# Starting three gate and value products of block 1 on three of its four tiles, and loading q and k of the next tiles ahead of the output weights

## The chip, the cores and the metric

The kernel runs on one core of a Trainium2 chip. The metric is the device time of one execution in microseconds (us): the median of three runs. A lower time is better. The core has a matrix engine (PE, with its weight loads shown apart as PEld), a vector engine (DVE), an activation engine (ACT), GpSimd (POOL), whose queue issues most of the loads here, and SyncE (SP), which issues stores and transposing transfers.

## The reference

An attention with a sliding window and a linear bias over the distance feeds a gated feed-forward block. The output of the attention, for 8 sequences of 576 tokens with 8 heads of 64, becomes a matrix x of 4608 tokens by 512.

```python
window = 128
scale = 1.0 / np.sqrt(D)
scores = scale * np.matmul(q, k.transpose(0, 1, 3, 2))
bias = slopes[:, None, None] * (-np.abs(rel))[None, :, :]
mask = (rel >= 0) & (rel < window)
scores = np.where(mask, scores + bias[None], -1e9)
attn = softmax(scores)                      # written out in the reference
x = np.matmul(attn, v)                      # then 4608 x 512
g = x @ w_gate                              # 512 x 1536
silu = g * (1.0 / (1.0 + np.exp(-g)))
out = (silu * (x @ w_val)) @ w_out          # 1536 x 512
```

## The kernel before

The tokens are cut into tiles of 128 (`unit` i, tile i), and four tiles make a block of 512 tokens, nine blocks in all. Attention works tile by tile, and the feed-forward part works block by block, some steps behind it. The two are written as generators that are advanced in turn, so that instructions of both alternate on each engine.

A tile of k or q is loaded by the POOL queue, turned on PE through the identity (`pt`, line 214) and copied out of PSUM by ACT (k) or DVE (q). Scores (`ps`, `psc`) take the turned k and q, ACT takes their exponential, DVE multiplies by the mask, and PE weighs v with it (`av`, line 350). DVE divides by the sum into `x`, PE turns `x` (`px`, line 376), and ACT copies it into `xT[n]`, the input of block n.

The gate and value products of a block are made by `wide`. Each has four matmuls over the 512 rows of the input, on up to 512 tokens of the block. A product can be done in two goes: first on the columns of the tiles that are there, and later on the rest, in the same PSUM buffer. The kernel before uses that for block 0 alone. The PSUM pool `ps_f` has three buffers under the tag `gv`.

```python
def wide(n, m, which, c1=512):                       # line 394
    w, ms = wg_sb if which == "g" else wv_sb, slice(m * P, (m + 1) * P)
    ps, c0 = early.pop((n, m, which), (None, 0))
    if ps is None:
        pool, tag = (ps_a, "a") if (n, m, which) in OTHER else (ps_f, "gv")
        ps = pool.tile([P, 512], FP32, name="p" + which, tag=tag)
    for kb in range(NKB):                            # 4
        nc.tensor.matmul(ps[:, c0:c1], w[:, kb, ms], xT[n][:, kb, c0:c1], ...)   # line 402
    if c1 < 512:
        early[(n, m, which)] = (ps, c1)
    return ps

def gate(n, m, pg, ...):                             # frees the gate's buffer
    nc.scalar.activation(tt, pg, AF.Tanh, scale=0.5)                   # line 420, ACT
    nc.vector.scalar_tensor_tensor(out=uu, in0=tt, ..., in1=pg, ...)   # line 421, DVE

def val(n, m, pv, ...):                              # frees the value's buffer
    nc.vector.tensor_mul(hT[n][:, m, ...], uu, pv)                     # line 432, DVE

def project(n, j, pool, tag, bufs):                  # output product of block 0, tile j
    po = pool.tile([P, DM], FP32, name="po", tag=tag, bufs=bufs)
    for m0 in range(0, NMB, 4):
        for i in range(m0, m0 + 4):
            m = NMB - 1 - i if n == 0 else i
            nc.tensor.matmul(po, hT[n][:, m, ...], wo_sb[:, m, :], ...)   # line 456
        ...
```

`project` for block 0 reads the second half of the output weights `wo_sb` first (m from 11 down). Its first tile has 12 matmuls, of which the first six use `wo_sb[:, 6:12]` and the others `wo_sb[:, 0:6]`. It follows the last product of block 0 in the program, while tiles 7 and 8 of the attention are under way. The feed-forward generator and the order of loads, cut:

```python
def ffn():
    for n in range(NBLK):
        ...
        if n == 1:
            for j in range(PRE):                     # PRE = 0
                ...
        for m in range(NMB):                         # 12
            for half, _ in enumerate(gate_val(n, m)):
                ...
            if n == 1:
                if m in (4, 6, 8, 10):
                    for _ in project(0, m // 2 - 2, ps_f, "po", 1):
                        yield 1.0
# ... cut ...
def begin(n, tiles):
    for m, which in ((0, "g"), (0, "v"), (1, "g"), (1, "v"), (2, "g"), (2, "v"))[:n]:
        if early.get((0, m, which), (None, 0))[1] < tiles * P:
            wide(0, m, which, tiles * P)
# ... cut: the loads, in the order of the POOL queue ...
load_w(1280, 1536)
load_v(7)
load(8)
nc.gpsimd.dma_start(wo_sb[:, 6:12, :], wo2[:, 6:12, :])
nc.gpsimd.dma_start(wo_sb[:, 0:6, :], wo2[:, 0:6, :])
load_qk(9)
load_qk(10, "q")
load_v(9)
load_qk(10, "k")
load_v(10)
```

The place of an instruction in its engine's queue is not that of the source alone: a list scheduler orders PE, DVE and ACT. The POOL queue keeps the order of the source.

Of the kernel before, what the change touches and what calls it, by code (L numbers as in the profile page):

```python
# [16 lines left out]
P = 128  # L17
# [33 lines left out]
def kernel(  # L51
# [117 lines left out]
    def source(src, rank):  # L169

        s, c = divmod(rank, 9)
        if c == 8:
            return [((64 * n, 64 * n + 64),
                     src[2 * s + n, :, 512:576, :].rearrange("h p d -> p h d")) for n in range(2)]
        b, t = 2 * s + c // 4, c % 4
        return [((0, P), src[b, :, t * P:(t + 1) * P, :].rearrange("h p d -> p h d"))]

    def load_v(rank):
        va[rank] = va_all[rank % NV]
        for (p0, p1), src in source(v, rank):  # L180
            nc.gpsimd.dma_start(va[rank][p0:p1, :, 0:D], src)  # L181

    def load_qk(rank, which="kq"):
        for name in which:
            t_ = nat.tile([P, H, D], FP16, name=name + "n", tag=name + "n")
            for (p0, p1), src in source(k if name == "k" else q, rank):
                nc.gpsimd.dma_start(t_[p0:p1], src)  # L187
            (natk if name == "k" else natq)[rank] = t_

    def load(rank):  # L190
        load_qk(rank)
        load_v(rank)
# [198 lines left out]
    early = {}  # L391
    OTHER = {(0, 0, "g"), (0, 0, "v"), (0, 1, "g"), (0, 1, "v")}

    def wide(n, m, which, c1=512):
# [6 lines that stand above are left out]
        for kb in range(NKB):  # L401
            nc.tensor.matmul(ps[:, c0:c1], w[:, kb, ms], xT[n][:, kb, c0:c1],  # L402
                             start=(kb == 0 and c0 == 0), stop=(kb == NKB - 1 and c1 == 512),
                             skip_group_check=(n == 0))
        if c1 < 512:
            early[(n, m, which)] = (ps, c1)
        return ps
# [26 lines left out]
    def gate_val(n, m):  # L434
        c0 = 384 if (n, m) in acted else 0
        gate(n, m, wide(n, m, "g"), c0)
        yield
        val(n, m, wide(n, m, "v"), c0)
        yield
# [11 lines left out]
    def project(n, j, pool, tag, bufs):  # L451
# [4 lines that stand above are left out]
                nc.tensor.matmul(po, hT[n][:, m, j * P:(j + 1) * P], wo_sb[:, m, :],  # L456
                                 start=(i == 0), stop=(i == NMB - 1))
            if m0 + 4 == NMB:
                osb = opool.tile([P, DM], FP32, name="osb", tag="osb")
                nc.scalar.mul(osb, po, 0.5)  # L460
                store(n, j, osb)
            yield
# [10 lines left out]
    def weight_sums(c):  # L473

        if c == 0:
            one_more.append(supool.tile([P, 1], FP32, name="one", tag="pin", bufs=1))
            nc.vector.memset(one_more[0], 1.0)
        k = slice(2 * c, 2 * c + 2)
        for t_, a, b in ((T1, B12, B11), (T3, B22, B12)):
            nc.vector.scalar_tensor_tensor(out=t_[:, k, :], in0=a[:, k, :], scalar=one_more[0],  # L480
                                           in1=b[:, k, :], op0=ALU.mult, op1=ALU.subtract)
        nc.vector.tensor_sub(T2[:, k, :], B22[:, k, :], T1[:, k, :])
        nc.vector.tensor_sub(T4[:, k, :], B21[:, k, :], T2[:, k, :])
# [11 lines left out]
    def at_once(fs):  # L495
        for f in fs:
            f()
# [208 lines left out]
    def ffn():  # L706

        for n in range(NBLK):
            if n > 1:
                parts = chain(strassen(n - 1, 0), strassen(n - 1, 1))  # L710
            if n == 1:
                for j in range(PRE):
                    for _ in project(0, j, ps_f, "po", 1):
                        yield 1.0
            if n == SEVEN_FROM:
                break
            due, given = 0, 0
            for m in range(NMB):
                for half, _ in enumerate(gate_val(n, m)):
                    scored[0] = False  # L720
                    yield 1.0
                    due += n > 1 and 2 * m + half in AT
                    while due and not (scored[0] and given % 7 == 1):
                        next(parts)
                        due, given = due - 1, given + 1
                        yield 0.75
                    if n > 1:
                        for _ in range(1 + (len(later) > 3)):
                            if later:
                                later.pop(0)()  # L730
# [4 lines that stand above are left out]
                    if m in (4, 6, 8):  # L735
                        weight_sums(m // 2 - 2)
                if n > 0 and m >= 9:
                    (at_once if n == 1 and m < 11 else later.extend)(sums(n, m - 9))
                if n + 1 == SEVEN_FROM:
                    if m == SILU_AT:  # L740
                        attention_ends()
                        by_silu.update((n, i) for i in range(m + 1, NMB))
                    if m in (SILU_AT + 1, SILU_AT + 2):
                        later.extend(gate_val_weight_sums(m - SILU_AT - 1))
                    if m == SILU_AT:
                        later.extend(x_sums(n + 1))
            if n > 1:
                assert next(parts, 0) == 0
        ends = [strassen(NBLK - 1, t) for t in range(2)]
        tail = ExitStack()  # L750
        for n, k, name, which in seven_steps():
            if k == 0 and n > SEVEN_FROM:
                assert next(parts, 0) == 0
                parts = chain(strassen(n - 1, 0), strassen(n - 1, 1))
            if n == SEVEN_FROM and k in (1, 3, 10, 17):
                later.extend(gate_val_weight_sums(2 + (k + 4) // 7))
            yield 0.5
            if k % 3 == 2 and k < 42:
                next(parts)
                yield 0.75  # L760
            if k == 20 and n + 1 < NBLK:
                later.extend(x_sums(n + 1))
            if k == 35:
                later.extend(sums(n, 0))
            if name == "fourth" and which is not None and which[1] > 3:
                if n + 1 < NBLK or k < 39:
                    later.extend(sums(which[0], which[1] - 3))
            for _ in range(2 if len(later) > 4 or k < 7 else 1):
                if later:
                    later.pop(0)()  # L770
            if n == NBLK - 1 and k == 38:
                at_once(later)
                later.clear()
                tail.enter_context(tc.manual_schedule(engines={ET.DVE}))
            if n == NBLK - 1 and k == 39:
                one, two = sums(n, 1), sums(n, 2)
                one[0]()
            if n == NBLK - 1 and k == 41:
                one[1]()
                next(ends[0])  # L780
                yield 0.75
            if n == NBLK - 1 and k == 42:
                two[0]()
        assert next(parts, 0) == 0 and not later
        at_once((two[1], one[2], two[2], one[3], two[3]))

        for t in (1, 0, 1, 0, 1, 0, 1, 0, 0, 1, 0, 1, 1):
            next(ends[t])
            yield 0.75
        tail.close()  # L790
# [25 lines left out]
                f()  # L816
            yield

    def begin(n, tiles):

        for m, which in ((0, "g"), (0, "v"), (1, "g"), (1, "v"), (2, "g"), (2, "v"))[:n]:
            if early.get((0, m, which), (None, 0))[1] < tiles * P:
                wide(0, m, which, tiles * P)

    def first_tiles():

# [83 lines left out]
    load_w(1280, 1536)  # L910
    load_v(7)
    load(8)
    nc.gpsimd.dma_start(wo_sb[:, 6:12, :], wo2[:, 6:12, :])
    nc.gpsimd.dma_start(wo_sb[:, 0:6, :], wo2[:, 0:6, :])
    load_qk(9)
    load_qk(10, "q")
    load_v(9)
    load_qk(10, "k")
    load_v(10)
# [94 lines left out]
```

The softmax here doesn't subtract the row's maximum and nothing guards it: scores larger than these inputs give would overflow.

## Time and profile before

| what | value |
|---|---|
| device time, median of 3 runs | 340.84 us (340.82 to 340.93) |
| span of the profiled execution | 339.4 us |
| PE busy | 328.6 us, 97% of the span |
| DVE busy | 274.7 us, 81% |
| ACT busy | 208.3 us, 61% |
| POOL busy | 109.7 us, 32% |

The page of the profile gives the busy time of each engine first, then the same in 40 slices of 8.5 us, each digit a share in tenths. The view of waits sums, for each instruction of an engine, the idle time before it by what ended it. The timeline lists instructions in order with start, duration and idle time before. A matmul's duration includes the passage through the array, which overlaps with the next matmul. So the pace of PE is read from the distance of two starts, and not from durations.

### The profile page before, as it was taken

The page shows a single profiled execution, that of the slowest core. Times are in us where ns is not written, and L with a number is a line of the kernel's source. Part 1 is how long each engine was busy: PE and PEld are TensorE (multiplying, and loading weights), DVE is VectorE, ACT ScalarE, POOL GpSimd, SP SyncE. Part 2 cuts the span into 40 slices and gives each one's busy share as a digit, 9 for nine tenths or more (in the row PEclk, how much of TensorE's full clock was granted, in tenths as well). Part 3 has the DMA queues.
Part 4 walks back from the last instruction along what each step waited for, and adds up shares of the span by engine and source line. Part 5 has one row for each costly group of instructions (what it writes and reads, how often), then busy time and mean ns, then how long its engine had stood idle before and what let it go on. Part 6 is the DMA issues. An engine that isn't in the chain of part 4 may idle for free.

```text
span 339.4 us, 7672 instructions
## 1 busy us (share of the span) xinstructions
PE 328.6 (97%) x2935; PEld 217.4 (64%) x2935; DVE 274.7 (81%) x643; ACT 208.3 (61%) x415; POOL 109.7 (32%) x136
## 2 busy tenths in 40 slices
PE   8999987999999999999999999999999999999994
PEld 4564444444455665566665655666688888888884
DVE  4668874999888779998899999999955885776683
ACT  4866774555575676666665647563467776776650
POOL 8977675377837068743008000000000000000000
PEclk9999999999999999999999999999999999999998
DMA  9999999999999999999939913021101101011014
GB/s 151 169 178 178 166 162 162 128 139 157 142 170 147 172 153 179 157 156 154 181 109 109 152 39 93 17 58 53 62 2 64 47 17 65 0 65 62 2 64 125
DMA packets 160037, 37.37 MB, mean 110 GB/s; under 512 B 147328, under 2 KB 155648, under 8 KB 160000
## 3 DMA queue, kind: packets, MB, share of 16 engines
q0 software_dynamic: 118336, 18.62, 80.3%
q1 hardware_dynamic: 40976, 17.64, 28.4%
q10 hardware_dynamic: 688, 0.62, 0.6%
q8 instruction: 23, 0.38, 0.5%
q14 instruction: 14, 0.11, 0.1%
HBM read 37.91 MB, written 9.44 MB: 139 GB/s over the span
## 4 chain that ended last, share of the span: by engine, by line
PE 79%; DMA 11%; POOL 4%; DVE 2%; ACT 2%; issue 1%; POOLq 0%
PE po L537 19%; PE pg L402 15%; PE pv L402 15%; PE gX L626 9%; DMA wv_sb<-in_moe_w_val_dram 5%; PE gY L626 5%; PE av L350 4%; DMA qn<-in_q_dram 3%; PE ps L282 3%; PE p L537 3%; DMA va<-in_v_dram 3%; PE gZ L626 2%; PE po L456 2%; POOL va L181 1%; PE px L376 1%
## 5 line engine op out<-in xcount | busy, mean ns | idle before, releaser
L402 PE MATMUL pv<-xT,wv_sb 128*128 128x512 f16 (+2 forms) x304 | 75.8, 368 | 0.3 <-DVE uu L421 0.3
L402 PE MATMUL pg<-xT,wg_sb 128*128 128x512 f16 (+2 forms) x304 | 75.1, 368 | 0.2 <-DVE xT L378 0.2
L420 ACT ACTIVATE tt<-pg 128x512 f16<-128x512 f32 x68 | 41.0, 603 | 47.2 <-PE pg L402 46.9
L288 ACT ACTIVATE ex<-ps 128x512 f16<-128x512 f32 x96 | 49.9, 606 | 7.5 <-PE ps L282 7.5
L421 DVE SCALAR_TENSOR_TENSOR uu<-tt,pg 128x512 f16<-128x512 f16 x67 | 45.6, 680 | 9.1 <-ACT tt L420 9.1
L432 DVE TENSOR_TENSOR hT<-uu,pv 128x512 f16<-128x512 f16 x68 | 46.2, 680 | 2.9 <-PE pv L402 1.3
L181 POOL DMA_DIRECT2D va<-in_v_dram x40 | 34.3, 865 | 42.3 <-PE av L350 34.6
L537 PEld LDWEIGHTS <-hT 128*128 128x128 f16 x384 | 37.2, 98 | 10.6 <-issue 0.8
L402 PEld LDWEIGHTS <-wv_sb 128*128 128x128 f16 x304 | 27.3, 98 | 24.8 <-issue 2.7
L402 PEld LDWEIGHTS <-wg_sb 128*128 128x128 f16 x304 | 27.3, 98 | 23.2 <-issue 1.9
L187 POOL DMA_DIRECT2D kn<-in_k_dram x39 | 33.3, 858 | 16.8 <-DMA qT<-qn 6.4
L187 POOL DMA_DIRECT2D qn<-in_q_dram x39 | 33.4, 865 | 12.6 <-DMA va<-in_v_dram 5.4
L537 PEld LDWEIGHTS <-S 128*128 128x128 f16 x288 | 27.4, 98 | 7.3 <-issue 1.4
L294 DVE TENSOR_TENSOR ex<-ex,m_reg 128x1024 f16<-128x1024 f16 x42 | 28.7, 685 | 2.6 <-ACT ex L288 2.5
L353 DVE TENSOR_TENSOR x<-av,rec 128x256 f16<-128x256 f32 x72 | 28.7, 419 | 0.4
L537 PE MATMUL po<-T,S 128*128 128x256 f16 x192 | 25.9, 273 | 0.3 <-ACT u2s L563 0.3
L537 PE MATMUL po<-T,hT 128*128 128x256 f16 x192 | 26.0, 272 | 0.0
L322 ACT ACTIVATE exc<-psc 128x512 f16<-128x512 f32 x40 | 21.3, 607 | 1.9 <-PE psc L318 1.9
L680 DVE TENSOR_TENSOR hT<-s,v 128x512 f16<-128x512 f16 x18 | 7.6, 424 | 17.7 <-ACT s L679 17.7
L350 PEld LDWEIGHTS <-ex 128*128 128x128 f16 x384 | 17.4, 97 | 3.9 <-issue 0.4
L350 PE MATMUL av<-va,ex 128*128 128x65 f16 x384 | 19.3, 193 | 0.0
L282 PE MATMUL ps<-qT,kT 64*128 64x256 f16 x192 | 16.9, 272 | 0.3 <-DVE qT L219 0.2
(130 smaller groups left out, 535.3 us busy)
## 6 DMA issues: line engine op xcount, KB each, us to landing
out_dram<-osb SPq DMA_DIRECT2D x32, 256.0 KB, 2.1
va<-in_v_dram POOLq DMA_DIRECT2D x32, 128.0 KB, 7.8
qn<-in_q_dram POOLq DMA_DIRECT2D x31, 128.0 KB, 8.1
kn<-in_k_dram POOLq DMA_DIRECT2D x31, 128.0 KB, 8.8
wg_sb<-in_moe_w_gate_dram POOLq DMA_DIRECT2D x6, 256.0 KB, 7.7
wv_sb<-in_moe_w_val_dram POOLq DMA_DIRECT2D x6, 256.0 KB, 8.1
wo_sb<-in_moe_w_out_dram POOLq DMA_DIRECT2D x2, 768.0 KB, 10.4
kn<-in_k_dram POOLq DMA_DIRECT2D x8, 64.0 KB, 6.0
```

Of the source, the lines that this page charges most:

```text
L181: nc.gpsimd.dma_start(va[rank][p0:p1, :, 0:D], src)
L187: nc.gpsimd.dma_start(t_[p0:p1], src)
L288: nc.scalar.activation(e[:, o:o + 2, :], banks[q4][par], AF.Exp, scale=scale)
L294: nc.vector.tensor_mul(e[:, o, :], e[:, o, :], reg[:, o, :])
L350: nc.tensor.matmul(av[:, j, :], w, val, start=(n == 0), stop=(n == len(todo) - 1))
L353: nc.vector.tensor_mul(x[:, 4 * half:4 * half + 4, :], av[:, :, 0:D], rec.broadcast_to([P, 4, D]))
L402: nc.tensor.matmul(ps[:, c0:c1], w[:, kb, ms], xT[n][:, kb, c0:c1], start=(kb == 0 and c0 == 0), stop=(kb == NKB - 1 and c1 == 512), skip_ ...
L420: nc.scalar.activation(tt, pg[:, c0:c1], AF.Tanh, scale=0.5)
L421: nc.vector.scalar_tensor_tensor(out=uu, in0=tt, scalar=one if (n, m) == PIN else 1.0, in1=pg[:, c0:c1], op0=ALU.add, op1=ALU.mult)
L432: nc.vector.tensor_mul(hT[n][:, m, c0:c1], acted[(n, m)][1][:, c0:c1], pv[:, c0:c1])
L537: nc.tensor.matmul(dst, a[:, m, cols], b[:, m, :], start=(start and m == 0), stop=(m == HM - 1), skip_group_check=True)
L626: nc.tensor.matmul(dst[:, i, :], w[:, kb, c0 + i * P:c0 + (i + 1) * P], a[:, kb, :], start=(start and i == 0 and kb == 0), stop=(i == 1 an ...
```

## The change

Three gate and value products of block 1 (gate 0, value 0, gate 1) are begun on the first three tiles of the block, at the head of its steps, before the fourth tile is there. They fill all three buffers of the tag `gv`. The rest, one tile of 128 columns each, follows when the fourth tile has been copied. The loads of q and k of tile 9, and of q of tile 10, move ahead of the two loads of the output weights. Both give PE something to do that depends neither on the output weights nor on the fourth tile. The third edit lets `wide` leave out a check of groups of accumulation, which is of the build alone.

```diff
@@ wide
-                             skip_group_check=(n == 0))
+                             skip_group_check=(n <= 1))
@@ ffn
             if n == 1:
+                begin(3, 3, 1)
                 for j in range(PRE):
@@ begin
-    def begin(n, tiles):
+    def begin(n, tiles, block=0):
 
         for m, which in ((0, "g"), (0, "v"), (1, "g"), (1, "v"), (2, "g"), (2, "v"))[:n]:
-            if early.get((0, m, which), (None, 0))[1] < tiles * P:
-                wide(0, m, which, tiles * P)
+            if early.get((block, m, which), (None, 0))[1] < tiles * P:
+                wide(block, m, which, tiles * P)
@@ loads
     load(8)
+    load_qk(9)
+    load_qk(10, "q")
     nc.gpsimd.dma_start(wo_sb[:, 6:12, :], wo2[:, 6:12, :])
     nc.gpsimd.dma_start(wo_sb[:, 0:6, :], wo2[:, 0:6, :])
-    load_qk(9)
-    load_qk(10, "q")
     load_v(9)
```

## The prediction

> **What bounds the kernel now.** I read the page first: busy time by engine, then the 40 slices.
>
> ```profile
> PE 328.6 (97%) x2935; PEld 217.4 (64%) x2935; DVE 274.7 (81%) x643; ACT 208.3 (61%) x415; POOL 109.7 (32%) x136
> ...
> PE   8999987999999999999999999999999999999994
> ...
> DMA  9999999999999999999939913021101101011014
> ```
>
> PE is the bound, and between the first and the last slice only the sixth and seventh (8.5 us each, so 42 to 59 us) dip. The DMA engines are busy there. The table of four windows shows how narrow the dip is (stretch, length, then busy us and count for PE, PEld, DVE, ACT, POOL, then clock, DMA share, GB/s).
>
> ```profile
> 40.00:49.00 9.00, 8.16 (x95) 4.47 (x95) 7.47 (x18) 6.69 (x13) 6.91 (x8) 1.00 1.50 150
> 49.00:57.00 8.00, 5.73 (x63) 3.11 (x58) 3.61 (x9) 4.14 (x9) 3.44 (x4) 1.00 1.96 172
> 57.00:76.00 19.00, 18.91 (x129) 8.59 (x127) 16.94 (x33) 10.66 (x20) 10.57 (x13) 1.00 1.88 136
> 76.00:95.00 19.00, 18.76 (x158) 8.95 (x157) 16.85 (x43) 11.39 (x22) 15.05 (x19) 1.00 2.19 151
> ```
>
> In 49 to 57 us PE is busy 5.73 of 8.00; DVE and ACT are under 4.2 as well. After 57 PE is full. Then the view of waits of PE:
>
> ```profile
> PE po L456 <- DMA wo_sb<-in_moe_w_out_dram: 1.3, 2, 1.0
> ...
> PE pt L214 <- DMA qn<-in_q_dram: 0.6, 1, 0.6
> ...
> PE pt L214 <- DMA kn<-in_k_dram: 0.3, 1, 0.3
> ```
>
> PE waits for the output weights (twice), then for k and q of tile 9. These are the only waits for a transfer in the whole span. The timeline of PE places them (start, duration, instruction, idle before it):
>
> ```profile
> 52.18 0.59 PE L456 MATMUL po<-wo_sb,hT 128*128 128x512 f16 x2
> 53.78 0.59 PE L456 MATMUL po<-wo_sb,hT 128*128 128x512 f16 x2 [1.01 <-DMA wo_sb<-in_moe_w_out_dram]
> 54.21 0.27 PE L376 MATMUL px<-idm,x 128*128 128x128 f16 x2
> 54.74 0.40 PE L214 MATMUL pt<-idm,kn 128*128 128x128 f16 x4 [0.26 <-DMA kn<-in_k_dram]
> 55.70 0.40 PE L214 MATMUL pt<-idm,qn 128*128 128x128 f16 x4 [0.56 <-DMA qn<-in_q_dram]
> 55.94 0.59 PE L456 MATMUL po<-wo_sb,hT 128*128 128x512 f16 x2
> 56.37 0.28 PE L376 MATMUL px<-idm,x 128*128 128x128 f16 x2
> 56.61 0.40 PE L214 MATMUL pt<-idm,qn 128*128 128x128 f16 x4
> 56.84 0.59 PE L456 MATMUL po<-wo_sb,hT 128*128 128x512 f16 x2
> 57.32 1.02 PE L402 MATMUL pg<-xT,wg_sb 128*128 128x512 f16 x4
> ```
>
> Block 1 begins at 57.32. By then all 12 `po` of tile 0 are done.
>
> **What the Trainium skill says.** "TensorE: Matmul & The Clock Gate", section "Back-to-back issue gap": start to start, a warm matmul takes its columns over 2.4 GHz plus 2.5 ns. The trace agrees. Products of four 512-column matmuls start 0.86 to 0.87 us apart (57.32, 58.18, 59.04), or 0.216 each. The 128-column rests of block 0 start 0.22 apart per four, or 0.055 each. So 384 and 128 columns cost what 512 cost, and cutting a product in two is free. "Perfetto Trace Analysis", section "Per-instruction lifecycle: what the profiler-reported window actually captures": a matmul's profiled end is a model. The listed idle is therefore too short by the tail, and I count from start to start. "DMA: Bandwidth & Descriptors", section "Queues, rings and completion order": an engine consumes a ring's descriptors in order. The trace fits this: the weights become ready before k and q of tile 9, as issued. No page tells what the new order of instructions costs.
>
> **The change part by part.**
>
> 1. *Stalls removed.* Start-to-start, with 0.216 per 512 columns and 0.055 per 128:
>    - second weights: 53.78 - (52.18 + 2 x 0.216) = 1.17
>    - k of tile 9: 54.74 - (54.21 + 0.11) = 0.42
>    - q of tile 9: 55.70 - (54.74 + 0.22) = 0.74
>    - first weights, at 49.97: seven small score matmuls from 49.34 end near 49.54, plus 0.1 for the step to 128-row matmuls (50.19 to 50.28 in the same rows), so 0.33
>
>    The sum is 2.66 us.
>
> 2. *Work moved.* By the order of the built program, 12 matmuls of 384 columns now stand among the scores and `av` of tiles 7 and 8, where nine of the 12 `po` stood. The nine `po` go behind them. 12 x 384 = 9 x 512 = 4608 columns, so PE's work up to the start of block 1 proper is the same. In all, 12 matmuls are added and no column.
>
> 3. *Do the new waits bite?* Walking the new order from 49.7 with those durations, PE reaches k of tile 9 at about 53.2 and the first `po` at 53.65. Loads: k, q, q took 0.96 each (54.74 to 55.70). The first weights came at 49.97 and the second 3.81 later, so the first started at 46.2 or before. In the new order k and q of tile 9 land by 47.1 and 48.1, and q of tile 10 by 49.1. The weights come 3 x 0.96 = 2.9 later, the first at 52.85, the second at 56.7. PE needs the first at 53.65: 0.8 us to spare. The second half is read only by the seventh `po`, which now stands behind five gate-value pairs, after 60. PE begins the rests at about 54.65, against 57.32.
>
> 4. *What is given back.* The fourth tile's copy by ACT (0.59) ends near 54.75: 0.15. Three products ready at once fill the three buffers. Value 1 waits until DVE has taken gate 0 (ACT 0.60, DVE 0.60): about 0.2. Gate 2 waits for value 0 behind both gates on DVE: about 0.3. Together 0.65 us. The scores of tile 9 stand in one run of eight where they were cut in three (61.73, 62.95, 65.97), each cut costing two steps of 0.1: two cuts fewer give 0.4.
>
> Sum: 2.66 - 0.65 + 0.4 = 2.4 us. By the walk, tile 8's `av` begins near 64.65 against 67.16: 2.5. From there PE is full to 325 us, so what it is ahead should reach the end. 340.84 - 2.4 = 338.4 us.
>
> **The rivals.**
>
> - *DVE takes it.* DVE is busy 33.8 of 38 us in 57 to 95, so a PE that is ahead could just wait for `uu` and `hT`. For it: three buffers in a ring and seven DVE waits in these rows. Against it: DVE idles 2.33 and 1.54 us before its first `uu` at 59.01 and starts about 3 us earlier too; work per product is unchanged. If it held, half the gain would go: 339.6.
> - *The weights come too late.* They were the first wait, and they now follow three transfers. If they landed 2 us later than my 52.85, PE would stall 1.2 us at the first `po` and k, q would still be early: 339.6.
> - *Later loads become the bound.* A PE that is ahead meets q and k sooner. Against it: the turning transfers of tile 11 are issued at 60.3 to 61.7 and take about 6.9, while its scores run from 72.2, so over 3 us are spare; POOL waits for PE (`av`, 34.6 us in all) later on, so loads run ahead. If it held, 340.8.
> - *The scheduler's new order shifts stalls far behind,* by a few tenths either way; the count of steps between 64-row and 128-row matmuls falls from 88 to 84, which is neutral.
>
> **Range and chances.** All rivals but the third leave a gain; the gain is capped by 2.66 + 0.4 = 3.1 (337.7). So the range is 337.6 to 340.1. Two per cent would be 6.8 us, over twice the cap: faster by over 2% 0.01, within 2% 0.98, slower by over 2% 0.01.
>
> **What would show it.** Right: PE's waits for `wo_sb`, k and q of tile 9 vanish or are under 0.2; PE in 49 to 57 us is busy over 7.3; the first rest of 128 columns starts at 54.5 to 55; PE waits for DVE of at most 0.5 appear behind it; tile 8's `av` starts 2 to 3 us earlier, and this lead holds to the end. Wrong: a stall for `wo_sb` at the first `po` (step 3), DVE waits over 1 us (step 4), or a lead at 65 us that is gone by 100 us (the third rival).

## The result and the profile after

The changed kernel takes 338.49 us (median of four runs, 338.32 to 338.92) against 340.88 us for the kernel before on the same chip. The ratio is 0.9931, with a 95% interval of 0.9914 to 0.9948. The prediction said 338.4 us.

The page of the changed kernel, busy time and slices of PE:

```profile
PE 327.1 (97%) x2947; PEld 218.1 (65%) x2947; DVE 273.8 (81%) x643; ACT 208.1 (62%) x415; POOL 109.8 (33%) x136
...
PE   7999989999999999999999999999999999999994
```

The dip of two slices has shrunk to one digit 8 (the 7 in front belongs to the start of the kernel), and PE has 12 matmuls more. The same stretches as in the prediction (the columns are as there):

```profile
49.00:57.00 8.00, 7.61 (x93) 4.88 (x93) 5.05 (x12) 6.12 (x13) 3.03 (x4) 1.00 1.37 193
57.00:76.00 19.00, 18.92 (x130) 9.15 (x131) 18.91 (x41) 10.06 (x19) 9.63 (x11) 1.00 1.86 126
76.00:95.00 19.00, 18.90 (x166) 9.40 (x166) 16.01 (x40) 12.60 (x24) 12.89 (x16) 1.00 2.30 144
```

In 49 to 57 us PE is busy 7.61 us where it was 5.73. In 57 to 76 DVE is now busy 18.91 of 19.00 (16.94 before), and PE is still full. The waits of PE in the changed kernel:

```profile
PE pt L208 <- DMA stage<-in_q_dram: 0.8, 1, 0.8
...
PE pv L402 <- DVE uu L421: 0.4, 2, 0.3
```

No wait for the output weights or for k and q of tile 9 is listed. The first line is a wait at the very start of the kernel, for a load that the change doesn't touch. It is there in this execution and leaves everything up to 49 us 0.24 us later than in the profile before: the seven small score matmuls start at 49.57 and not 49.34. The timeline of PE where the stalls were:

```profile
49.57 0.38 PE L318 MATMUL psc<-qT,kT 64*128 64x128 f16 x7 [0.20 <-ACT xT L380]
...
53.53 0.39 PE L214 MATMUL pt<-idm,qn 128*128 128x128 f16 x4
53.94 0.38 PE L456 MATMUL po<-wo_sb,hT 128*128 128x512 f16 x1
...
54.48 0.59 PE L456 MATMUL po<-wo_sb,hT 128*128 128x512 f16 x2
55.10 0.38 PE L402 MATMUL pg<-xT,wg_sb 128*128 128x128 f16 x4
...
56.40 0.39 PE L456 MATMUL po<-wo_sb,hT 128*128 128x512 f16 x1
56.95 1.02 PE L402 MATMUL pv<-xT,wv_sb 128*128 128x512 f16 x4 [0.16 <-DVE uu L421]
...
64.73 0.89 PE L350 MATMUL av<-va,exc 128*128 128x65 f16 x24
...
240.40 0.60 PE L626 MATMUL gX<-xT,wg_sb 128*128 128x256 f16 x4
...
331.63 0.82 PE L537 MATMUL po<-T,hT 128*128 128x256 f16 x6
```

The same four places in the timeline of the kernel before:

```profile
49.34 0.38 PE L318 MATMUL psc<-qT,kT 64*128 64x128 f16 x7 [0.19 <-ACT xT L380]
...
67.16 0.89 PE L350 MATMUL av<-va,exc 128*128 128x65 f16 x24
...
243.12 0.60 PE L626 MATMUL gX<-xT,wg_sb 128*128 128x256 f16 x4
...
334.37 0.82 PE L537 MATMUL po<-T,hT 128*128 128x256 f16 x6
```

The rests of 128 columns start at 55.10, where block 1 started at 57.32. Tile 8's `av` starts at 64.73 against 67.16, which is 2.43 us earlier. The stage that makes gates and values by seven products (`gX`, line 626) starts at 240.40 against 243.12, and the last run of matmuls at 331.63 against 334.37, so the lead stays, at 2.72 and 2.74. With the late start put back, the change is worth nearly 3 us in this pair of profiles. The spans differ by 2.6 us and the medians by 2.39. The start differs between executions.

### The profile page after: what moved, and what is told of

It reads as the page before. It is cut to its first block, busy times and chain, and to the rows that moved or that the text cites. A ratio compares the mean times of both kernels' runs of the same rounds, so it can differ in the third digit from the quotient of the medians.

```text
span 336.8 us, 7693 instructions
## 1 busy us (share of the span) xinstructions
PE 327.1 (97%) x2947; PEld 218.1 (65%) x2947; DVE 273.8 (81%) x643; ACT 208.1 (62%) x415; POOL 109.8 (33%) x136
## 4 chain that ended last, share of the span: by engine, by line
PE 88%; DVE 4%; ACT 4%; DMA 2%; issue 1%; SPq 0%; DVEq 0%
PE po L537 19%; PE pg L402 17%; PE pv L402 17%; PE gX L626 9%; PE gY L626 5%; PE av L350 4%; PE ps L282 4%; PE po L456 3%; PE p L537 3%; PE gZ L626 2%; PE px L376 2%; DMA stage<-in_q_dram 2%; PE psc L318 1%; DVE uu L421 1%; ACT tt L420 1%; ACT ex L288 1%
## 5 line engine op out<-in xcount | busy, mean ns | idle before, releaser
L402 PE MATMUL pv<-xT,wv_sb 128*128 128x512 f16 (+3 forms) x308 | 76.0, 365 | 0.5 <-DVE uu L421 0.4
L402 PE MATMUL pg<-xT,wg_sb 128*128 128x512 f16 (+3 forms) x312 | 76.0, 363 | 0.2 <-DVE xT L378 0.2
```

## The experiments

The order of instructions on PE, DVE and ACT doesn't depend on the order of the loads in these kernels. Where a run changes only the loads, the three engines have the order of the kernel that it is made from. Three sets of runs were made, each with its own runs of the kernel before (340.47, 340.56 and 340.57 us). Ratios are to those.

### The two halves of the change, each alone

The begun products without the new order of loads:

```diff
-    load_qk(9)
-    load_qk(10, "q")
     nc.gpsimd.dma_start(wo_sb[:, 6:12, :], wo2[:, 6:12, :])
     nc.gpsimd.dma_start(wo_sb[:, 0:6, :], wo2[:, 0:6, :])
+    load_qk(9)
+    load_qk(10, "q")
```

> Only the three begun products; the loads in the order of before. PE, DVE and ACT have the order of the changed kernel. My theory (both halves of the change are needed): k and q of tile 9 and q of tile 10 land at about 54.7, 55.7 and 56.6 us as before, but PE now reaches k of tile 9 at 53.3, so it waits 1.4 + 0.7 + 0.5 us there and starts the rests of block 1 near 57.3: 340.4 to 341.0 us, no gain. Rival (the begun products alone fill the gap, the loads' move is cosmetic): 338.3 to 339.2 us.

It took 340.08 us, ratio 0.9989 (0.9981 to 0.9997). The timeline of PE in this kernel:

```profile
54.06 0.40 PE L214 MATMUL pt<-idm,kn 128*128 128x128 f16 x4 [0.72 <-DMA kn<-in_k_dram]
55.04 0.40 PE L214 MATMUL pt<-idm,qn 128*128 128x128 f16 x4 [0.58 <-DMA qn<-in_q_dram]
...
55.96 0.40 PE L214 MATMUL pt<-idm,qn 128*128 128x128 f16 x4 [0.19 <-DMA qn<-in_q_dram]
```

The stall for the weights has gone, and PE waits for k and q instead, three times. Most of the gain is lost (0.4 us of 2.4 are left). The time is 0.3 us below the range expected: k of tile 9 was there 0.7 us earlier than in the profile before (54.06 against 54.74), though it was issued at the same time (43.14 and 43.12). Why it landed earlier is not known.

The new order of loads without the begun products:

```diff
             if n == 1:
-                begin(3, 3, 1)
```

> Only the loads moved; no products begun, so PE has the order of before and its first output product stands at 49.7 us. My theory: the weights land at 53.9 and 58.5 as in the changed kernel, so PE waits about 4 us at the first output product and again at the seventh, and block 1 starts near 60.7 where it started at 57.3: 343.5 to 344.6 us, slower than before. Rival (the gain comes from q and k being early, waits of 0.42 + 0.74 us): 339.5 to 339.9 us.

It took 345.14 us, ratio 1.0131 (1.0115 to 1.0147). The first output product in its timeline:

```profile
54.08 0.59 PE L456 MATMUL po<-wo_sb,hT 128*128 128x512 f16 x1 [4.43 <-DMA wo_sb<-in_moe_w_out_dram]
```

Two stretches of its table of windows (the last three columns are the granted clock, the DMA share and GB/s):

```profile
49.00:57.00 8.00, 3.37 (x28) 1.60 (x25) 1.56 (x3) 3.38 (x7) 3.37 (x4) 0.61 1.33 195
57.00:76.00 19.00, 18.97 (x131) 9.36 (x129) 14.21 (x31) 8.02 (x15) 9.62 (x11) 0.90 1.89 132
```

PE stood for 4.43 us, from 49.65 to 54.08, and the granted clock was 0.61 and 0.90 in these stretches, where it was 1.00 in every other kernel here. Cut finer, the same view has 1.00 in 49 to 50 us, 0.84 in 50 to 51, 0.50 in 51 to 60, 0.54 in 60 to 61 and 1.00 after. So the clock fell near 50.7, while PE stood, and rose near 60.9. Four output matmuls at 57.94 take until 59.63, 0.42 each and not 0.216. Half the clock from 54.08 to 60.9 costs at most 3.4 us (an estimate: half of 6.8). That is more than the 0.5 us by which the time is above the range, but PE would have spent a part of it waiting for the second half of the weights, which came near 57.9 (issue at 45.40 and 12.5 to landing). How much of the loss is the clock was not separated. So the begun products alone gain 0.4 us, the loads alone lose 4.7, and together they gain 2.4: the loads remove the waits that the begun products uncover, and the begun products cover the time that the weights lose.

### When the weights land

Gate 0 and value 0 begun once more, ahead of that, on two tiles. This gives PE more work near 47 us, where it waits for `x` of tile 6:

```diff
+                begin(2, 2, 1)
                 begin(3, 3, 1)
```

> The changed kernel with gate 0 and value 0 of block 1 begun once more ahead of that on the first two tiles, so that these 256 columns fill PE's wait for x of tile 6 near 47.1 to 47.7 us. My theory: the transfer of the weights sets the pace at the first output product. PE gets there near 52.6, 0.6 us earlier than the order of work alone, and waits until they land at 53.9, with three more products in front of q and k of tile 9: about 1 us slower than the changed kernel, 339.2 to 340.0 us. Rival (PE's own work sets the pace, every filled gap is gained): 337.7 to 338.1 us.

It took 339.25 us, ratio 0.9965 (0.9954 to 0.9976). The line of its first output product:

```profile
54.14 0.81 PE L456 MATMUL po<-wo_sb,hT 128*128 128x512 f16 x3 [1.92 <-DMA wo_sb<-in_moe_w_out_dram]
```

PE is busy 8.91 of 9.00 us in 40 to 49, where it was 8.17, and then waits 1.92 us for the weights. More work ahead of a transfer that sets the pace gave nothing. It even lost about 1 us against the changed kernel, as expected: three output products now stand ahead of k and q of tile 9 and hold them up too, so that the rests of 128 columns start at 56.51 and not at 55.10.

The changed kernel, with the first half of the weights first again:

```diff
+    nc.gpsimd.dma_start(wo_sb[:, 6:12, :], wo2[:, 6:12, :])
     load_qk(9)
     load_qk(10, "q")
-    nc.gpsimd.dma_start(wo_sb[:, 6:12, :], wo2[:, 6:12, :])
     nc.gpsimd.dma_start(wo_sb[:, 0:6, :], wo2[:, 0:6, :])
```

> The changed kernel with the first half of the weights (the one that the first output products read) loaded ahead of q and k of tile 9 again, and the second half behind q of tile 10. The engines' order is that of the changed kernel. My theory: in the changed kernel the first output product waits some 0.2 us for weights that land at 53.9, hidden in the modelled end of the matmul before; here they land at 49.9, k and q of tile 9 at 50.9 and 51.9, q of tile 10 at 52.9, all before PE wants them: 338.1 to 338.4 us, 0.1 to 0.3 faster than the changed kernel. Rival (the weights were in time in the changed kernel): 338.4 to 338.6 us, the same.

It took 338.16 us, ratio 0.9932 (0.9919 to 0.9944). This ratio can't be told from the changed kernel's. The same two steps in its timeline:

```profile
53.25 0.39 PE L214 MATMUL pt<-idm,qn 128*128 128x128 f16 x4
53.47 0.38 PE L456 MATMUL po<-wo_sb,hT 128*128 128x512 f16 x1
```

The step is 0.22 us, four matmuls at 0.055. In the changed kernel it was 0.41 (53.53 to 53.94), so 0.19 us of waiting stood there that no list shows. The profiles show it; the times are too coarse for it.

Both of the last two together, that is, the two tiles first and the first half of the weights first:

> Gate 0 and value 0 begun on two tiles ahead of the three products on three tiles, and the first half of the weights loaded ahead of q and k of tile 9 again. My theory (without the wait for the weights, 1.9 us in the run with the two tiles alone, PE's own work sets the pace and a filled gap is gained): PE's wait for x of tile 6, 0.77 us, is filled, 0.6 to 0.8 us faster than with the half of the weights first alone, 337.2 to 337.7 us, ratio to before 0.990 to 0.992. Rival (PE ahead of DVE gives the gain back in waits for the gates and values of block 1): 338.0 to 338.3 us.

It took 337.38 us, ratio 0.9910 (0.9897 to 0.9924). On the same chip the changed kernel itself took 338.40 us:

> The changed kernel itself, as the measure for the three others of this set on the same chip: 338.0 to 338.6 us, ratio to before 0.993.

Its ratio is 0.9942 (0.9930 to 0.9955). The version with both is 1.0 us faster than the changed kernel on that chip, and the fastest here. Against the same order of instructions with the weights late (0.9965, 0.9954 to 0.9976) the intervals lie apart. It has no wait for the weights and none for `x` of tile 6.

The opposite, v of tile 9 and k of tile 10 also ahead of the weights:

```diff
     load_qk(10, "q")
+    load_v(9)
+    load_qk(10, "k")
     nc.gpsimd.dma_start(wo_sb[:, 6:12, :], wo2[:, 6:12, :])
     nc.gpsimd.dma_start(wo_sb[:, 0:6, :], wo2[:, 0:6, :])
-    load_v(9)
-    load_qk(10, "k")
```

> The changed kernel with v of tile 9 and k of tile 10 also loaded ahead of the weights; the engines' order is the changed kernel's. The prediction's second rival, made on purpose. Theory (the landing of the first half of the weights sets the start of the output products): they land 1.9 to 2.1 us later, near 55.8, PE waits about 2 us at the first output product, 340.1 to 340.7 us, and nearly all of the gain is gone. Rival (PE has other work there, or the transfers were not in line): 338.4 to 339.2 us.

It took 340.23 us, ratio 0.9999 (0.9985 to 1.0014). The first output product in its timeline:

```profile
55.41 0.38 PE L456 MATMUL po<-wo_sb,hT 128*128 128x512 f16 x1 [1.73 <-DMA wo_sb<-in_moe_w_out_dram]
```

The weights came 1.5 us later, and the time is that of the kernel before. The profile shows only a part of this loss: `gX` starts at 241.92, which is 1.52 us behind the changed kernel and still 1.20 ahead of the kernel before. By the ratios 1.9 to 2.3 us of the gain went. The rest is not explained.

### What is given back behind, and what a cut costs

Two begun products and not three, on the kernel with the first half of the weights first:

```diff
-                begin(3, 3, 1)
+                begin(2, 3, 1)
```

> Two products begun instead of three (gate 0, value 0), with the first half of the weights first, so that no weights are waited for. My theory: what was given back in the prediction were waits for DVE because three products become ready at once (0.16 and 0.3 us in the changed kernel), and what was won were two cuts fewer in the scores of tile 9 (0.2 us each). Here the waits go and the cuts come back: 338.0 to 338.5 us, within 0.2 of the same kernel with three. Rival (the third product is needed as work while PE waits): 338.6 to 339.0 us.

It took 338.77 us, ratio 0.9951 (0.9935 to 0.9966). That lies above my range and within the rival's. But the interval overlaps those of the same kernel with three (0.9919 to 0.9944) and of the changed kernel, so the times don't show the rival either. PE's listed waits of a value for DVE's gate fall from 0.4 us in two places to 0.3 in one, and the scores of tile 9 are cut in three again. Counted in the traces, PE's steps between 64-row and 128-row matmuls are 88 in the kernel before, 84 with three begun products and 88 with two. One pair of profiles gives a size: from the seven small score matmuls (49.57 here, 49.29 with three) to tile 8's `av` (64.85 and 64.26) the kernel with two takes 0.31 us more, and to `gX` (240.53 and 239.92) 0.33 more. The medians, from two chips, differ by 0.6. So the third product was worth about 0.3 us in the profiles; the times leave its size open.

All 96 products of blocks 2 to 5 cut into 384 and 128 columns, in the changed kernel:

```diff
-        for kb in range(NKB):
-            nc.tensor.matmul(ps[:, c0:c1], w[:, kb, ms], xT[n][:, kb, c0:c1], ...)
+        for a, b in ([(c0, 384), (384, c1)] if 2 <= n <= 5 else [(c0, c1)]):
+            for kb in range(NKB):
+                nc.tensor.matmul(ps[:, a:b], w[:, kb, ms], xT[n][:, kb, a:b], ...)
```

> The changed kernel with all 96 gate and value products of blocks 2 to 5 cut into 384 and 128 columns, 384 more matmuls and no more columns. Theory (a cut is free): 338.2 to 338.8 us, as the changed kernel. Rival (each matmul pays its fixed 2.5 ns, 384 of them about 1 us, with PE the bound): 339.2 to 339.8 us. A weight load that no longer hides behind 128 columns would cost more: over 341 us.

It took 340.80 us, ratio 1.0009 (1.0001 to 1.0017), 2.4 us more than the changed kernel on that chip. A cut product takes 0.87 to 0.88 us (150.76 to 151.63, 157.57 to 158.45) and an uncut one 0.86. Its profile also had a wait of 0.7 us for the weights, which belongs to no cut. So the same cuts were made on the kernel with the first half of the weights first:

> All 96 gate and value products of blocks 2 to 5 cut, as in the run before of that kind, but with the first half of the weights first, so that its wait of 0.7 us for them cannot occur. Theory (of the 2.4 us that the cuts cost there, 0.7 was that wait, about 1.0 are 384 fixed costs of 2.6 ns, and the rest are waits for DVE in the new order): 339.4 to 340.2 us. Rival (the cuts alone cost 2.4 us): 340.4 to 341.0. Rival (only the fixed cost): 339.0 to 339.3.

It took 340.48 us, ratio 0.9994 (0.9986 to 1.0002). That is outside my range and at the edge of the rival's: without that wait the cuts still cost 2.3 us by the medians (338.16 uncut, on another chip) and 2.1 by the ratios. The profiles have 2.12: from the seven small score matmuls to `gX` 242.15 - 49.40 against 239.92 - 49.29. Two stretches of the windows of the cut kernel:

```profile
150.00:200.00 50.00, 49.68 (x585) 37.31 (x583) 46.26 (x111) 29.72 (x61) 12.84 (x16) 1.00 1.58 146
200.00:243.00 43.00, 42.27 (x464) 31.92 (x463) 42.04 (x105) 21.06 (x42) 0.00 (x0) 1.00 0.19 53
```

The same stretches of the uncut kernel with the same loads:

```profile
150.00:200.00 50.00, 49.97 (x463) 30.24 (x462) 46.70 (x114) 29.45 (x61) 13.71 (x17) 1.00 1.64 148
200.00:243.00 43.00, 42.96 (x365) 26.53 (x363) 42.09 (x105) 23.19 (x46) 0.00 (x0) 1.00 0.21 56
```

PE idles 0.29 + 0.69 = 0.98 us more in these two stretches. Its list of waits has 0.9 us for DVE's gates in three places, where the uncut kernel has 0.4 in two, and a new 0.3 for `x`. Of the remaining 1.1 us in the profiles, 1.0 is busy time: a cut product takes 873 ns to the next instruction and an uncut one 863 (medians of 79 and 89 such products in the two traces), which is 10 ns for four matmuls more, or 2.5 ns each, and 384 x 2.5 ns = 0.96 us. The Trainium skill ("TensorE: Matmul & The Clock Gate", "Back-to-back issue gap") gives the same 2.5 ns as the fixed part of the gap of an isolated warm matmul. Its 131 ns for 512 columns in a stream of weight loads and matmuls is not what these traces show: the step is 216 ns. That the idle time comes from the new order of instructions, and not from the cuts themselves, was argued and not tried. A cut is not free, in any case.

## Why the prediction was right, step by step

1. *Stalls removed, 2.66 us.* Right. No listed wait for the output weights or for k and q of tile 9 is left. One stall was not counted: the turning of q of tile 10 at 56.61 stood 56.61 - (56.37 + 0.11) = 0.13 us late in the old timeline. The lead at tile 8's `av` is 2.43 us in the profiles, and 2.67 with the 0.24 us of the late start put back, where 2.5 was worked out. That the two edits are needed together was not said; the two runs with one alone show it.
2. *Work moved at no cost.* Right in the count, 2935 matmuls to 2947. "Cutting a product in two is free" is wrong: each further matmul costs 2.5 ns. Twelve of them are 0.03 us here; 384 are about 1 us.
3. *The weights land at 52.85, with 0.8 us to spare.* This step failed in its size. They set the first output product at 53.94, and PE had been ready at 53.53 + 0.22 = 53.75: 0.19 us too late, not 0.8 us early. With this wait and the late start (0.24) the rests begin at 55.10 and not at 54.65, just outside the 54.5 to 55 that the prediction named as a sign. The term was "3 x 0.96 = 2.9 later"; it measured 53.94 - 49.97 = 3.97, of which 0.24 is the late start. I took the pace at which transfers land in a full queue. What moved more was the issue. The POOL timeline of the kernel before shows the old places:

```profile
40.67 0.84 POOL L913 DMA_DIRECT2D wo_sb<-in_moe_w_out_dram  x1 [0.77 <-DMA wv_sb<-in_moe_w_val_dram]
...
43.99 1.77 POOL L187 DMA_DIRECT2D qn<-in_q_dram  x2
```

In the changed kernel k stands in the first place:

```profile
40.89 0.89 POOL L187 DMA_DIRECT2D kn<-in_k_dram  x1 [0.96 <-PE ps L282]
42.50 1.75 POOL L187 DMA_DIRECT2D qn<-in_q_dram  x2 [0.72 <-DMA kn<-in_k_dram]
44.24 0.84 POOL L916 DMA_DIRECT2D wo_sb<-in_moe_w_out_dram  x1
```

The issue is 3.57 us later, and issue to landing took 9.7 us against 9.3. With 9.3 us added to the fourth place of the old queue (43.99), the old profile would have given 53.3. In all twelve kernels the first half took 7.9 to 9.3 us from issue to landing where it stood first, and 9.1 to 9.9 where it stood behind three or five of these loads. So the later place costs mainly its issue slots, and some slower landing on top (0.4 us in this pair). In the prediction's own terms, q of tile 10 landed at 47.68 (43.37 at issue, 4.31 to landing) and not at 49.1, but the first weights came 6.2 us behind it and not 3.81. DMA moved 52 GB/s in 47 to 48 us, then 130 and 158, and about 205 from 50 us on; the pace of the second half, which came behind other transfers without a pause, was taken for the first. The order of landing held as the prediction took it. The section of the skill that it names states this order under the queues of SP and ACT; for POOL's queue the profile before shows it: the second weights, k and q of tile 9, issued at 42.30, 43.12 and 43.99, were there at 53.78, 54.74 and 55.70.
4. *Given back, 0.65 us.* Near in the sum by luck, and wrong in its parts. The copy of the fourth tile costs 55.10 - (54.48 + 0.43) = 0.19 (0.15 said). Value 1's wait for DVE is 56.95 - (56.40 + 0.22) = 0.33 (0.2 said). Gate 2 follows at 57.81, right behind it: none (0.3 said). That is 0.52; only with the 0.19 of step 3, which this step did not have, does it make 0.71. The 0.4 for the scores fits the timeline, where all eight stand in one run at 55.86, and the count of four steps fewer; the run with two products didn't settle its size.
5. *The lead reaches the end.* Right: 2.43 at 65 us, 2.72 at 240, 2.74 at the end. The last 0.3 was not foreseen. A listed wait of 0.24 us for `x` at 86.58 of the old timeline has gone; which change of order did that was not tried. This is the fourth rival, the scheduler's new order, and it was worth some tenths in favour of the change.

Of the other rivals, DVE took 0.33 us and no more, although it is full in 57 to 76 us; later loads never became the bound (the lead grew from 65 us to the end); the late weights were real, by 0.19 us, and decisive once they were put later still.

## What to carry to other kernels

When an engine stands at several transfers in a row, list what it would reach next after each is removed: one half of such a change alone gained 0.4 us, the other lost 4.7, and both together gained 2.4. A transfer that is moved back in an issuing queue is late by its issue slots, so read the old issue times of the slot that it moves to and add its own time from issue to landing; here that gives 53.3 us, where 53.9 was measured and 52.85 predicted. Where a load has two halves with different first uses, try putting only the second one back: this removed 0.19 us in the changed kernel, which the times can't show, and was worth 1.9 us (0.9965 to 0.9910) once PE had been given more work ahead.

## What the runs showed of the hardware

An idle stretch of PE of 4.43 us went with a granted clock of 0.50 from near 50.7 to near 60.9 us, and matmuls of 512 columns then took 0.42 us each. Idle stretches of 1.92 and 1.73 us left it at 1.00. The Trainium skill ("TensorE: Matmul & The Clock Gate", "Part 1: The HAM clock gate") says that PE's clock is halved after at least one idle window of about 3.4 us. The halving is seen here. The idle time that it takes is not confirmed: the clock was recorded as halved about 1 us after PE stopped, and a stretch of 1.92 us elsewhere did not halve it. A listed idle time of zero can hide a real wait: 0.19 us stood between 53.53 and 53.94, where the matmul before is shown as 0.39 us long and the step without a wait is 0.22. Start-to-start distances show it. Each matmul more cost 2.5 ns at the same number of columns.
